# First token block of a gated attention/SwiGLU kernel: three of its four x tiles transposed by DMA instead of on TensorE

## The chip, the core and the metric

The kernel runs on one core of a Trainium2 chip, in one launch. The metric is the device time of the execution in microseconds (us). The median of several executions is the number that counts. The profiler recorded one execution, and all durations below come from that record.

## The reference, cut to what matters

The input x has 2048 tokens of 512 numbers (bf16). A linear attention block and a SwiGLU block both read it, and a gate per token mixes them:

```python
qkv = x @ wqkv                                  # 512 -> 3*512, 32 heads of 16
phi = lambda t: jnp.where(t > 0, t + 1, jnp.exp(t)) + 1e-6
pq, pk = phi(q), phi(k)
kv  = jnp.einsum("bhsd,bhse->bhde", pk, v)      # summed over all tokens
z   = jnp.einsum("bhsd->bhd", pk)
num = jnp.einsum("bhqd,bhde->bhqe", pq, kv)
den = jnp.einsum("bhqd,bhd->bhq", pq, z)[..., None] + 1e-6
a   = (num / den) @ wo
b   = (silu(x @ w1) * (x @ w3)) @ w2            # inner width 1376
g   = sigmoid((x * gate_w).sum(-1, keepdims=True))
out = g * a + (1 - g) * b
```

All of q cannot be used before k of every token has been seen, because kv and z are sums over all 2048 tokens.

## The kernel before, in words

The tokens are cut into 16 tiles of 128 (`P`) and four blocks of 512 (`TB`), so that a block has four tiles (`TPB`). The inner dimension of 512 is cut into four chunks of 128 (`KC`).

x is held twice in SBUF. `x_sb` is token-major: tokens on the partitions. `xT` is the transposed copy: the inner dimension on the partitions. A k, q, gate or up projection needs `xT`. The product `XP` (x transposed times phi(k), accumulated over all 16 tiles, from which kv comes) needs `x_sb` and phi(k).

The whole order on TensorE is written out by hand (`manual_schedule` for that engine). The start of it, which the change touches, goes so:

- `emit_warm` issues matmuls on constants ("dummies", 128 by 512, result unused). Six of them stand at the very start of TensorE's stream and two more after the first transposes.
- `emit_xT(t)` (L164 to L176) transposes tile t of the first block on TensorE: four 128x128 transposes into PSUM, two halves; DVE copies the first half to `xT` (L174) and ACT the second (L176).
- `emit_k_mm` (L178) is one of the four matmuls of k of a tile, `emit_k_phi` (L184) turns k into phi(k) on ACT and DVE and adds it to a running sum on POOL. In the first block the transposes of tiles 1 to 3 stand between the k matmuls of tiles 0 to 2.
- After the first block a loop over tiles 4 to 15 takes turns: `emit_xp(u)` (four XP matmuls of an earlier tile) and then `emit_k(t)`. So XP of tile 0 comes right before k of tile 4.

The loads are issued from two queues. The ACT queue issues the two halves of the k weights `wk_sb` (L84), then ACT loads its function table and runs a first small activation (`pre`, L88). The SP queue (`dq`) issues, strictly in order: `x_sb` tile 0 (L81), `x_sb` tile 1 (L85), `x_sb` tiles 2 and 3 (L86), and then for each of blocks 1 to 3 a DMA transpose of 512 tokens straight from DRAM into `xT` (L90) followed by the token-major copy of the same block (L94). All other weights come behind these on SP (L97 to L109): the q weights, the remainder columns with the gate, the v weights, w1, w3, wo, w2. Nothing in this stretch of the SP queue waits for a compute engine.

Later stages are: q of block 0, the last XP, kv and its product with wo, then per block the SwiGLU matmuls (`emit_ffn`), the projections of the next block, and the outputs (`emit_out`). There SP also issues DMA transposes of 128 tokens out of SBUF: `hTr` (L266) and `pqT` (L290).

Of the kernel before, what the change touches and what calls it, by code (L numbers as in the profile page):

```python
# [17 lines left out]
def kernel(  # L18
# [12 lines left out]
    nc = tc.nc  # L31
    P = nc.NUM_PARTITIONS
# [7 lines left out]
    TB = 512  # L40
    NTB = S // TB
    TPB = TB // P
# [6 lines left out]
    x2d = A_x.flatten_outer_dims()  # L49
# [14 lines left out]
    x_sb = consts.tile([P, NT, D], BF16, name="x_sb")  # L64
    xT = consts.tile([P, KC, S], BF16, name="xT")
# [13 lines left out]
    x_r = x2d.rearrange("(t p) d -> p t d", p=P)  # L79
    dq = nc.sync  # L80
    dq.dma_start(out=x_sb[:, 0:1, :], in_=x_r[:, 0:1, :])  # L81
    for i in range(2):
        kcs = slice(2 * i, 2 * i + 2)
        nc.scalar.dma_start(out=wk_sb[:, kcs, :], in_=wqkv_r[:, kcs, D : 2 * D])  # L84
    dq.dma_start(out=x_sb[:, 1:2, :], in_=x_r[:, 1:2, :])  # L85
    dq.dma_start(out=x_sb[:, 2:TPB, :], in_=x_r[:, 2:TPB, :])  # L86
    pre = consts.tile([1, 1], FP32, name="pre")
    nc.scalar.activation(out=pre[:], in_=nc.const_aps.tensor(0.0, [1, 1], FP32), func=ACT.Exp)  # L88
    for tb in range(1, NTB):
        dq.dma_start(  # L90
            out=xT[:, :, tb * TB : (tb + 1) * TB], in_=x2d[tb * TB : (tb + 1) * TB, :],
            transpose=True,
        )
        dq.dma_start(  # L94
            out=x_sb[:, tb * TPB : (tb + 1) * TPB, :], in_=x_r[:, tb * TPB : (tb + 1) * TPB, :]
# [4 lines left out]
    with nc.allow_non_contiguous_dma(reason="one gate weight per partition and chunk"):  # L100
        dq.dma_start(
            out=wr_sb[:, :, 2 * FR : NR], in_=gate_w.rearrange("(kc d o) -> d kc o", d=P, o=1)
# [14 lines left out]
        out=bm, in_=bm, pattern=[[-Dh, HPC], [0, Dh]], compare_op=ALU.is_ge, fill=0.0,  # L117
# [3 lines left out]
        out=bm, in_=bm, pattern=[[Dh, HPC], [0, Dh]], compare_op=ALU.is_ge, fill=0.0,  # L121
# [13 lines left out]
    def phi(dst, ps):  # L135
        e = work.tile([P, D], BF16, tag="phi_e", name="phi_e")
        e_ins = nc.scalar.activation(out=e[:], in_=ps, func=ACT.Exp)  # L137
        em = work.tile([P, D], BF16, tag="phi_m", name="phi_m")
        nc.vector.tensor_scalar(  # L139
            out=em[:], in0=e[:], scalar1=1.0, scalar2=1e-6, op0=ALU.min, op1=ALU.add  # L140
        )
        nc.vector.scalar_tensor_tensor(  # L142
            out=dst, in0=ps, scalar=0.0, in1=em[:], op0=ALU.max, op1=ALU.add
        )
        return e_ins
# [9 lines left out]
    def emit_warm(n):  # L155
        warm = psX.tile([P, TB], FP32, tag="XP3", name="warm")
        for i in range(n):
            nc.tensor.matmul(warm[:], lhsT=warm_l, rhs=warm_r, start=True, stop=True)

    emit_warm(6)  # L160

    st = {}

    def emit_xT(t):  # L164
        for h in range(2):
            xTp = psX.tile([P, 2, P], BF16, tag=f"XP{(2 * t + h) % 3}", name="xTp")
            for j in range(2):
                kc = 2 * h + j
                nc.tensor.transpose(  # L169
                    out=xTp[:, j, :], in_=x_sb[:, t, kc * P : (kc + 1) * P], identity=ident[:]  # L170
                )
            xT_t = xT[:, 2 * h : 2 * h + 2, t * P : (t + 1) * P]
            if h == 0:
                nc.vector.tensor_copy(out=xT_t, in_=xTp[:])  # L174
            else:
                nc.scalar.activation(out=xT_t, in_=xTp[:], func=ACT.Copy)  # L176

    def emit_k_mm(k_ps, t, kc):  # L178
        nc.tensor.matmul(  # L179
            k_ps[:], lhsT=xT[:, kc, t * P : (t + 1) * P], rhs=wk_sb[:, kc, :],  # L180
            start=(kc == 0), stop=(kc == KC - 1),
        )

    def emit_k_phi(k_ps, t):  # L184
        e_ins = phi(pk_sb[:, t, :], k_ps[:])
        if t == 0:
            nc.gpsimd.tensor_copy(pks[:], pk_sb[:, t, :])
        else:
            nc.gpsimd.tensor_add(pks[:], pks[:], pk_sb[:, t, :])  # L189
# [172 lines left out]

    k0 = [psM.tile([P, D], FP32, tag="mm", name=f"k0_{t}") for t in range(TPB)]
    emit_xT(0)
    emit_warm(2)
    emit_k_mm(k0[0], 0, 0)
    emit_k_mm(k0[0], 0, 1)
    emit_xT(1)
    emit_k_mm(k0[0], 0, 2)
    emit_k_mm(k0[0], 0, 3)  # L370
    emit_k_phi(k0[0], 0)
    emit_xT(2)
    for t in range(1, TPB):
        for kc in range(KC):
            emit_k_mm(k0[t], t, kc)
        emit_k_phi(k0[t], t)
        if t == 1:
            emit_xT(3)


    XP_ps = [psX.tile([P, D], FP32, tag=f"XP{dc}", name=f"XP{dc}") for dc in range(KC)]
# [21 lines left out]
    for c in range(KC):  # L403
# [7 lines left out]
        out=kvT_sb[:], in0=kvT_ps[:],  # L411
# [70 lines left out]
```

## Time and profile before

| what | us |
|---|---|
| median of 8 executions | 180.93 |
| lowest, highest | 180.63, 181.74 |
| the profiled execution | 180.89 |
| its span, first to last instruction | 179.1 |
| TensorE (PE) busy | 175.0, 98% of the span |
| VectorE (DVE) busy | 117.8 |
| ScalarE (ACT) busy | 66.8 |
| GpSimd (POOL) busy | 61.4 |

The profiled execution took 1.8 us more than its span: that is what lies around the first and last instruction. The rows of the profile name the line of the kernel, the engine, the operation, the tile written and the tile read. "SPq" and "ACTq" are the DMA-issuing instructions of those engines: their duration is the time that the issuing engine is held, and "us to landing" is from the start of the issue until the data is reported as arrived. A matmul's duration is modelled [...]; the distance from one start to the next is the better measure of its cost. In the chain of waits the pieces of PE stand end to end, so that a piece is listed about 0.16 us after the start of its first matmul.

### The profile page before, as it was taken

Reading aid. Unit: us, or ns where it says so; the run is one execution under the profiler, and the core shown is the slowest. Engines: PE = TensorE matmul, PEld = TensorE weight load, DVE = VectorE, ACT = ScalarE, POOL = GpSimd, SP = SyncE. Lnnn points to the kernel's source line nnn. Section 1 sums busy time; section 2 is a strip of 40 time slices with the busy share of each in tenths; the row PEclk is TensorE's granted clock in tenths of the full one; section 3 lists DMA queues with packets and bytes.
Section 4 is the critical chain, followed back from the end, with each engine's and each line's share of the span. In section 5 each row is a group of like instructions: output and inputs, shape, how many; then the busy total and the mean of one; then the engine's idle time right before and its main releaser. Section 6 shows DMA issues by size and latency. Waiting matters only on the chain.

```text
span 179.1 us, 2484 instructions
## 1 busy us (share of the span) xinstructions
PE 175.0 (98%) x892; PEld 84.1 (47%) x892; DVE 117.8 (66%) x205; ACT 66.8 (37%) x126; POOL 61.4 (34%) x69
## 2 busy tenths in 40 slices
PE   8999999999999999999999999999999999999993
PEld 3444444474444545444444444444545444444462
DVE  1578867697998837398787375978754669776000
ACT  4642322666523333342334343332433323341221
POOL 5186575646353323263003232620032328100000
PEclk9999999999999999999999999999999999999998
DMA  5999999901005010114000111240001023200011
GB/s 175 265 257 218 230 318 399 346 28 28 9 15 104 0 48 29 44 47 99 0 4 2 42 35 38 59 90 5 0 7 59 14 65 63 59 0 0 29 51 42
DMA packets 28286, 14.88 MB, mean 83 GB/s; under 512 B 19601, under 2 KB 27249, under 8 KB 28273
## 3 DMA queue, kind: packets, MB, share of 16 engines
q1 hardware_dynamic: 27728, 14.20, 29.4%
q10 hardware_dynamic: 544, 0.52, 0.9%
q8 instruction: 7, 0.11, 0.3%
q14 instruction: 7, 0.05, 0.1%
HBM read 8.42 MB, written 2.10 MB: 59 GB/s over the span
## 4 chain that ended last, share of the span: by engine, by line
PE 95%; DMA 2%; SPq 0%; DVE 0%; issue 0%; DVEq 0%
PE gate_ps L302 19%; PE o_ps L345 19%; PE up_ps L308 19%; PE o_ps L336 8%; PE XP L199 8%; PE q_ps L212 8%; PE k_ps L179 6%; PE r_ps L236 3%; DMA x_sb<-in_A_x_dram 2%; PE o_ps L340 2%; PE k L179 1%; PE kvT_ps L406 0%; PE W_ps L433 0%; PE xTp L169 0%; SPq L85 0%; SPq L81 0%
## 5 line engine op out<-in xcount | busy, mean ns | idle before, releaser
L302 PE MATMUL gate_ps<-xT,w_sb 128*128 128x512 bf16 x160 | 41.1, 379 | 0.0
L308 PE MATMUL up_ps<-xT,w_sb 128*128 128x512 bf16 x160 | 41.1, 379 | 0.0
L220 POOL TENSOR_TENSOR qz<-pq,z_sb 128x512 f32<-128x512 bf16 x16 | 18.5, 1161 | 60.6 <-DVE pq L142 58.7
L313 ACT ACTIVATE th<-gate_ps 128x512 bf16<-128x512 f32 x40 | 23.9, 597 | 38.4 <-PE gate_ps L302 38.0
L345 PE MATMUL o_ps<-w_sb,hT 128*128 128x512 bf16 (+2 forms) x180 | 37.5, 355 | 0.0
L315 DVE SCALAR_TENSOR_TENSOR gs<-th,gate_ps 128x512 bf16<-128x512 bf16 x40 | 27.3, 683 | 6.0 <-ACT th L313 5.7
L318 DVE TENSOR_TENSOR hT<-up_ps,gs 128x512 bf16<-128x512 f32 x40 | 27.6, 691 | 3.8
L139 DVE TENSOR_SCALAR phi_m<-phi_e 128x512 bf16<-128x512 bf16 x32 | 13.4, 419 | 20.7 <-ACT phi_e L137 20.5
L345 PEld LDWEIGHTS <-hT 128*128 128x128 bf16 x180 | 16.8, 97 | 17.9
L308 PEld LDWEIGHTS <-w_sb 128*128 128x128 bf16 x160 | 15.6, 98 | 19.0 <-issue 0.2
L302 PEld LDWEIGHTS <-w_sb 128*128 128x128 bf16 x160 | 15.6, 98 | 18.9 <-issue 0.3
L350 ACT ACTIVATE o_out<-o_ps,omg 128x512 bf16<-128x512 f32 (+2 forms) x17 | 11.1, 656 | 30.4 <-PE o_ps L345 30.4
L285 POOL TENSOR_TENSOR pqn<-pq,rden 128x512 bf16<-128x512 bf16 x16 | 16.6, 1056 | 14.0 <-DVE rden L278 11.7
L189 POOL TENSOR_TENSOR pks<-pks,pk_sb 128x512 f32<-128x512 f32 x15 | 17.5, 1167 | 8.9 <-DVE pk_sb L142 8.4
L223 DVE TENSOR_REDUCE den<-qz 128x32 f32<-128x512 f32 x16 | 11.0, 685 | 8.9 <-POOL qz L220 8.9
L336 PE MATMUL o_ps<-W_sb,pqT 128*128 128x512 bf16 (+2 forms) x72 | 16.8, 355 | 0.0
L212 PE MATMUL q_ps<-wq_sb,xT 128*128 128x512 bf16 x64 | 16.3, 379 | 0.0
L199 PE MATMUL XP<-pk_sb,x_sb 128*128 128x512 bf16 x64 | 16.1, 379 | 0.0
L137 ACT ACTIVATE phi_e<-k_ps 128x512 bf16<-128x512 f32 x12 | 7.2, 597 | 15.3 <-PE k_ps L179 15.3
L179 PE MATMUL k_ps<-wk_sb,xT 128*128 128x512 bf16 x48 | 12.3, 379 | 0.0
L137 ACT ACTIVATE phi_e<-q_ps 128x512 bf16<-128x512 f32 x16 | 9.6, 597 | 7.0 <-PE q_ps L212 5.8
L142 DVE SCALAR_TENSOR_TENSOR pq<-q_ps,phi_m 128x512 bf16<-128x512 f32 x16 | 11.1, 691 | 0.5
(59 smaller groups left out, 119.4 us busy)
## 6 DMA issues: line engine op xcount, KB each, us to landing
w_sb<-in_B_w_dram SPq DMA_DIRECT2D x3, 1280.0 KB, 9.6
out_dram<-o_out SPq DMA_DIRECT2D x15, 128.0 KB, 1.7
x_sb<-in_A_x_dram SPq DMA_DIRECT2D x3, 512.0 KB, 4.5
wk_sb<-in_A_wqkv_dram ACTq DMA_DIRECT2D x2, 256.0 KB, 3.5
wq_sb<-in_A_wqkv_dram SPq DMA_DIRECT2D x1, 512.0 KB, 6.6
wv_sb<-in_A_wqkv_dram SPq DMA_DIRECT2D x1, 512.0 KB, 6.6
wo_sb<-in_A_wo_dram SPq DMA_DIRECT2D x1, 512.0 KB, 10.6
x_sb<-in_A_x_dram SPq DMA_DIRECT2D x2, 128.0 KB, 2.8
```

The costliest lines, as they stand in the source:

```text
L179: nc.tensor.matmul(k_ps[:], lhsT=xT[:, kc, t * P : (t + 1) * P], rhs=wk_sb[:, kc, :], start=(kc == 0), stop=(kc == KC - 1),)
L189: nc.gpsimd.tensor_add(pks[:], pks[:], pk_sb[:, t, :])
L199: nc.tensor.matmul(XP_ps[dc][:], lhsT=x_sb[:, t, dc * P : (dc + 1) * P], rhs=pk_sb[:, t, :], start=(t == 0), stop=(t == NT - 1),)
L212: nc.tensor.matmul(q_ps[:], lhsT=xT[:, kc, ts_tok], rhs=wq_sb[:, kc, :], start=(kc == 0), stop=(kc == KC - 1),)
L220: nc.gpsimd.tensor_tensor(out=qz[:], in0=st[tb, "pq"][:, tt, :], in1=z_sb[:], op=ALU.mult)
L302: nc.tensor.matmul(gate_ps[:], lhsT=w1_sb[:, kc, fsl], rhs=xT[:, kc, tok_sl], start=(kc == 0), stop=(kc == KC - 1),)
L308: nc.tensor.matmul(up_ps[:], lhsT=w3_sb[:, kc, fsl], rhs=xT[:, kc, tok_sl], start=(kc == 0), stop=(kc == KC - 1),)
L313: nc.scalar.activation(out=th[:], in_=gate_ps[:], func=ACT.Tanh, scale=0.5)
L315: nc.vector.scalar_tensor_tensor(out=gs[:], in0=th[:], scalar=1.0, in1=gate_ps[:], op0=ALU.add, op1=ALU.mult)
L318: nc.vector.tensor_tensor(out=st[tb, "hT"][:, fc, :], in0=up_ps[:], in1=gs[:], op=ALU.mult)
L336: nc.tensor.matmul(o_ps[:], lhsT=st[tb, "pqT"][:, c, tsl], rhs=W_sb[:, c, a:b], start=(c == 0), stop=False,)
L345: nc.tensor.matmul(o_ps[:], lhsT=st[tb, "hT"][:, fc, tsl], rhs=w2_sb[:, fc, a:b], start=False, stop=(fc == FC - 1),)
```

## The change

Tiles 1 to 3 of the first block no longer go through TensorE. In the SP queue, the two loads of `x_sb` tiles 1 to 3 are replaced by two DMA transposes from DRAM into `xT`, of 128 tokens (tile 1) and of 256 tokens (tiles 2 and 3). The token-major copies of the three tiles become one DMA of 384 tokens on the ACT queue. It is written behind `emit_xT(0)`, and on ACT's own stream it stands behind `pre` and ahead of ACT's copy of tile 0's second half. The twelve TensorE transposes of tiles 1 to 3 and their six copies go away. The dummies go from six to five at the start and from two to one after tile 0's transposes. k of tiles 0 to 3 is then issued in one plain loop.

```diff
-    dq.dma_start(out=x_sb[:, 1:2, :], in_=x_r[:, 1:2, :])
-    dq.dma_start(out=x_sb[:, 2:TPB, :], in_=x_r[:, 2:TPB, :])
+    dq.dma_start(out=xT[:, :, P : 2 * P], in_=x2d[P : 2 * P, :], transpose=True)
+    dq.dma_start(out=xT[:, :, 2 * P : TB], in_=x2d[2 * P : TB, :], transpose=True)
...
-    emit_warm(6)
+    emit_warm(5)
...
     emit_xT(0)
-    emit_warm(2)
-    emit_k_mm(k0[0], 0, 0)
-    emit_k_mm(k0[0], 0, 1)
-    emit_xT(1)
-    emit_k_mm(k0[0], 0, 2)
-    emit_k_mm(k0[0], 0, 3)
-    emit_k_phi(k0[0], 0)
-    emit_xT(2)
-    for t in range(1, TPB):
+    nc.scalar.dma_start(out=x_sb[:, 1:TPB, :], in_=x_r[:, 1:TPB, :])
+    emit_warm(1)
+    for t in range(TPB):
         for kc in range(KC):
             emit_k_mm(k0[t], t, kc)
         emit_k_phi(k0[t], t)
-        if t == 1:
-            emit_xT(3)
```

## The prediction

> **What bounds the kernel now.** I read the page's first part, then the chain of waits for the first 20 us, then SP's own timeline with the rows of its DMAs.
>
> ```profile
> PE 175.0 (98%) x892; PEld 84.1 (47%) x892; DVE 117.8 (66%) x205; ACT 66.8 (37%) x126; POOL 61.4 (34%) x69
> ```
> ```profile
> 1.73 4.23 DMA x_sb<-in_A_x_dram
> 5.96 0.05 issue
> 6.01 0.40 PE xTp L169 x4
> 6.40 0.86 PE k L179 x4
> 7.27 0.22 PE xTp L169 x4
> 7.49 1.73 PE k L179 x8
> 9.22 0.86 PE XP L199 x4
> 10.08 0.86 PE k_ps L179 x4
> 10.94 0.86 PE XP L199 x4
> ```
>
> TensorE is the bound: in the chain of waits there is nothing but PE from 6.01 us on, matmuls end to end at 0.86 us per four. The last wait of PE is for `x_sb` tiles 2 and 3, issued at 1.73 and landed 4.23 us later. What is gained or lost before k of tile 4 (10.08 in the chain; its first matmul starts at 9.92 in the timeline) moves the end one for one, if nothing later begins to wait. So the whole question is: when can k of tile 4 start?
>
> That tile needs the DMA transpose of block 1, which is behind the changed lines on SP:
>
> ```profile
> 0.80 0.40 SPq L81 DMA_DIRECT2D x_sb<-in_A_x_dram  x1
> 1.26 0.42 SPq L85 DMA_DIRECT2D x_sb<-in_A_x_dram  x1
> 1.73 0.43 SPq L86 DMA_DIRECT2D x_sb<-in_A_x_dram  x1
> 2.20 3.52 SPq L90 DMA_TRANSPOSE xT<-in_A_x_dram  x1
> 5.77 0.58 SPq L94 DMA_DIRECT2D x_sb<-in_A_x_dram  x1
> 6.40 3.64 SPq L90 DMA_TRANSPOSE xT<-in_A_x_dram  x1
> ```
> ```profile
> L90 SPq DMA_TRANSPOSE xT<-in_A_x_dram x3: 3525/3641/3895, 2.2 to 10.7; - x3
> DMA to landing us min/median/max: 5.5/5.7/5.9
> ...
> L290 SPq DMA_TRANSPOSE pqT<-pqn x16: 1195/1216/1251, 52.2 to 153.0; - x16
> ...
> DMA to landing us min/median/max: 2.4/2.4/3.0
> ```
>
> SP is held 0.4 us by a plain load, but 3.5 to 3.9 us by a transpose of 512 tokens, and 1.2 us by one of 128 (`pqT`, from SBUF). Each 512-token transpose lands about 2.0 us after its issue has ended (5.5 - 3.525, 5.7 - 3.641, 5.9 - 3.895), whatever else was moving. So the issue, not the bandwidth, sets the landing. Today block 1 lands at 2.20 + 5.5 = 7.7, which leaves 2.2 us until 9.92.
>
> **The change part by part.**
>
> *TensorE work removed.* Two warm matmuls, twelve transposes. In the chain the transposes of tiles 2 and 3 are 0.40 + 0.22; tile 1's stand at 4.76 to 5.20, where k of tile 0 waits anyway: its third matmul starts at 5.20, and the second half of `wk_sb`, issued at about 1.29 with up to 3.9 us to landing, arrives just there. The dummies fill time before tile 0's data (landed at 0.80 + 2.5 = 3.3), so they cover a wait and are worth nothing. The wait at 6.0 goes. New stream: k of tile 0 ends its last two matmuls at 5.20 + 0.43 = 5.63, tile 1 follows to 6.50, tiles 2 and 3 to 8.22, XP of tile 0 to 9.08. PE could start k of tile 4 at 9.08: by itself a gain of 0.84 us. DVE loses three 0.29 us copies and ACT three of 0.38, all off the chain.
>
> *SP.* Two loads (0.42 + 0.43 us) go, two transposes come. Their cost is the deciding unknown. A line through 128 tokens = 1.22 and 512 = 3.64 gives 0.41 + 0.81 per 128 tokens: 1.22 for tile 1, 2.02 for tiles 2 and 3. Low end: cost in proportion to tokens, 3.525 / 4 = 0.88 and 1.76. High end: two pieces of 1.22 for the second, 2.45. Block 1's transpose then starts at 1.26 + 1.22 + 0.05 + 2.02 + 0.05 = 4.60 instead of 2.20 (low 4.00, high 5.03), and lands 5.5 to 5.9 later: 10.3 with the median. The matmul behind a landed load started 0.05 us after it (5.96 to 6.01), with a new weight load some 0.1 at most. So k of tile 4 starts at about 10.37, not at 9.08: PE waits 1.3 us there, and against 9.92 the sum is **+0.45**; with the shortest landing (5.5) +0.25, with the low price of the issues -0.3 to +0.1, with the high one up to +1.1. I take +0.35: between the median and shortest landing, since the transpose that was first on SP took 5.5.
>
> [...] 3.5 us against 0.58 for the same 512 KB on the same queue (L90 and L94). I go by the rows.
>
> *What is hidden by that 1.3 us wait.* Tile 1's piece (2.4 to 3.0 us by the `pqT` row) lands at 3.7 to 4.3, before 5.63. Tiles 2 and 3, issued at 2.53 and done at 4.55, land 1.2 to 2.0 us later, 5.8 to 6.6, perhaps 7.2 if their data share the DMA engines with the 384 KB from ACT, which follow `wk_sb` on ACT's queue. k of tile 2 wants them at 6.50; even 7.2 only moves XP of tile 0 to 9.8, still ahead of 10.37. ACT's new issue at 3.31 holds it for about 0.5 us (L86 and L94: 0.43 and 0.58) and so delays nothing; the dearest plain issue that I find in the trace, 2.47 us for `wv_sb` in a full queue, would hold ACT's copy of tile 0 until 6.2 and k of tile 0 until 6.7, XP of tile 0 then ends at 10.1, again under the cover. The loads from ACT land by about 8 (3.3 + 4.5) and XP of tile 1 reads them after 11. Without that cover each of these would cost its own lateness.
>
> *What is late next on SP.* Everything behind shifts by 2.4 us. Block 2's transpose would land at 14.6 (k of tile 8 starts about 17), block 3's at 19; block 1's `x_sb` at 12.8 (needed at about 16); the q weights at 24.3 (31.7); v weights 26.9 (38.2); w1 30.5 and w3 33.8 (39 and 40); wo 35.3 (43); w2 39.2 (60). SP comes free at 32.7 and its next work is ready at 39.6. All hold, so nothing is added. The copies of the three tiles on DVE and ACT and the running sum on POOL only get more room.
>
> **The sum.** The profiled execution took 180.89 (span 179.1 and 1.8 around it); plus 0.35 is 181.24, and the median stands 0.04 above that execution: 181.3.
>
> **The rivals.**
> *The short pieces are cheap to issue (gain).* No row shows a short transpose from DRAM; the 1.22 is from SBUF. If both pieces together took less than about 2.1 us, block 1 would land before 9.1 and the kernel would gain towards its floor of -0.84: 180.1. Against it: `hTr`, a quarter of the bytes of `pqT`, holds SP just as long (1.20), so a large part is a price per token or per instruction, and three 512-token issues agree to 10%. Chance 0.12, counting only gains over 0.3%.
>
> *The clock comes late (loss).* Matmuls start 0.43 us apart until 3.4 and 0.22 apart from 4.1 on: TensorE begins at half speed. The granted clock in the profile's rows says 1.00 throughout, so it cannot show the switch; the starts do. Before, PE is busy without a break from 0.84 to the switch. Now five dummies end at 2.97 and tile 0's data come at 3.37; 0.4 us are idle, 0.5 more follow before 5.2, and more at tile 2. [...] By the starts the switch stays at 4.1. [...] Chance 0.13.
>
> *The issues cost more than the line says,* by the high end or because the first transposes queue beside `wk_sb`: landing at 10.7 to 10.9, +0.8 to +1.1, so 181.7 to 182.0. Chance 0.25.
>
> **How the numbers follow.** The main case (k of tile 4 waits for block 1 at about 10.1 to 10.45, -0.1 to +0.55) has the remaining 0.50. About 0.3% (0.54 us) is what a measurement of this kernel can tell from no change. The main case counts for "same" but for a few hundredths at its upper edge; the two losses count as slower, with a few hundredths of their lower edge back in "same". Faster 0.12, same 0.48, slower 0.40. Likeliest time 181.3. The range from 180.4 to 182.2 leaves out most of the late-clock case and the lower part of the gain.
>
> **What would show it.** In SP's timeline: the two new issues at about 1.2 and 2.0 us and block 1's transpose starting near 4.6. In PE's waits: one for the DMA of `xT`, about 1.3 us, right before k of tile 4, which starts near 10.3; from there on the same unbroken stream as before. I am wrong in the gain's direction if block 1 is issued before 3.7, and in the other if matmuls after 8 us still start 0.43 apart, or if a second wait for DMA shows up behind tile 4.

## The result, and the profile after

The changed kernel is slower: a median of 184.85 us in 12 executions (181.56 to 186.16) against 181.14 for the kernel before (33 executions, 180.63 to 181.76). The ratio is 1.01, 95% interval 1.0073 to 1.0127; it leaves out the executions more than 1.5% above the fastest, which is why it is smaller than the medians say (184.85 / 181.14 = 1.02). The executions differ among themselves by 4.6 us, and those of the kernel before by 1.1. That spread is part of the answer. The first profile is of one of the long executions (185.84 us, span 184.0).

Its chain of waits for the first 30 us:

```profile
1.26 7.28 DMA xT<-in_A_x_dram
8.53 0.05 issue
8.58 5.29 PE k L179 x12
13.87 0.86 PE XP L199 x4
14.73 0.86 PE k_ps L179 x4
15.59 0.86 PE XP L199 x4
```

The last wait is no longer for block 1 but for tile 1's transpose, the one of 128 tokens: issued at 1.26, landed 7.28 us later. Then twelve k matmuls take 5.29 us. Before, they started 0.22 us apart, 2.6 us for twelve. k of tile 4 begins at 14.57 in the timeline instead of 9.92: +4.65 of the +4.95 us between the two profiled executions. From there on the stream has no wait for a DMA, as before; the other 0.3 us lie somewhere behind and are not accounted for.

TensorE's own timeline, and its waits in the first 12 us. In a row of the timeline, the brackets have the idle time before it and what ended that; in a row of the waits, the numbers are us in total, how often, and the longest:

```profile
3.89 1.01 PE L179 MATMUL k<-wk_sb,xT 128*128 128x512 bf16 x2
6.38 1.01 PE L179 MATMUL k<-wk_sb,xT 128*128 128x512 bf16 x2 [1.48 <-DMA wk_sb<-in_A_wqkv_dram]
8.58 5.29 PE L179 MATMUL k<-wk_sb,xT 128*128 128x512 bf16 x12 [1.19 <-DMA xT<-in_A_x_dram]
```
```profile
PE k L179 <- DMA wk_sb<-in_A_wqkv_dram: 1.5, 1, 1.5
PE k L179 <- DMA xT<-in_A_x_dram: 1.2, 1, 1.2
```

There are two new waits, 1.5 us for the second half of the k weights and 1.2 us for tile 1, and behind them the matmuls run at half speed (0.43 us from start to start instead of 0.22). They did so ahead of the waits too: the first two k matmuls, from 3.89 on, took 1.01 us together, against 0.59 for the two at 4.33 in the kernel before. The queues:

```profile
0.80 0.40 SPq L81 DMA_DIRECT2D x_sb<-in_A_x_dram  x1
1.26 1.29 SPq L85 DMA_TRANSPOSE xT<-in_A_x_dram  x1
2.60 1.29 SPq L86 DMA_TRANSPOSE xT<-in_A_x_dram  x1
3.94 4.93 SPq L90 DMA_TRANSPOSE xT<-in_A_x_dram  x1
```
```profile
0.80 0.98 ACTq L84 DMA_DIRECT2D wk_sb<-in_A_wqkv_dram  x2
1.81 1.28 ACT L88 ACT_TABLE_LOAD   x1 [1.81 <-issue]
1.87 0.44 ACTq L365 DMA_DIRECT2D x_sb<-in_A_x_dram  x1
```

SP issues the two pieces in 1.29 us each, and block 1 at 3.94. ACT issues the token-major load at 1.87, while its table load is still running, and not behind `pre` at 3.3. So the 384 KB are on their way almost together with tile 1's transpose. The view by microsecond shows what follows; after the stretch and its length stand the busy time of PE, its weight loads, DVE, ACT and POOL, then the granted clock, the busy share of the DMA engines and GB/s:

```profile
4.00:5.00 1.00, 0.90 (x3) 0.15 (x1) 0.00 (x0) 0.02 (x1) 0.00 (x0) 1.00 1.13 190
5.00:6.00 1.00, 0.00 (x0) 0.00 (x0) 0.00 (x0) 0.00 (x0) 0.00 (x0) 1.00 1.06 79
6.00:7.00 1.00, 0.62 (x2) 0.10 (x1) 0.00 (x0) 0.00 (x0) 0.00 (x0) 1.00 1.07 154
```

The engines are counted as busy (1.06 to 1.13) but move 79 to 190 GB/s, where plain loads in the kernel before went at 366 and 380 (3 to 5 us). The clock column says 1.00 throughout, although the matmuls start 0.43 us apart until 13.6 us, twice the 0.22 of full speed.

### The profile page after: what moved, and what is told of

Read it like the earlier page. It is cut to its first block, busy times and chain, and to the rows that moved or that the text cites. A ratio compares the mean times of both kernels' runs of the same rounds, so it can differ in the third digit from the quotient of the medians.

```text
span 184.0 us, 2451 instructions
## 1 busy us (share of the span) xinstructions
PE 177.4 (96%) x878; PEld 83.9 (46%) x878; DVE 118.7 (64%) x202; ACT 65.8 (36%) x123; POOL 61.2 (33%) x69
## 4 chain that ended last, share of the span: by engine, by line
PE 94%; DMA 4%; SPq 0%; DVE 0%; issue 0%; DVEq 0%
PE gate_ps L302 19%; PE o_ps L345 19%; PE up_ps L308 19%; PE XP L199 8%; PE o_ps L336 8%; PE q_ps L212 8%; PE k_ps L179 6%; DMA xT<-in_A_x_dram 4%; PE r_ps L236 3%; PE k L179 3%; PE o_ps L340 2%; PE kvT_ps L398 0%; PE W_ps L425 0%; SPq L81 0%; DVE o_out L354 0%
## 5 line engine op out<-in xcount | busy, mean ns | idle before, releaser
L139 DVE TENSOR_SCALAR phi_m<-phi_e 128x512 bf16<-128x512 bf16 x32 | 15.2, 475 | 26.9 <-ACT phi_e L137 26.9
L179 PEld LDWEIGHTS <-xT 128*128 128x128 bf16 x64 | 6.8, 108 | 13.1 <-issue 4.7
```

The source lines that it names most:

```text
L179: nc.tensor.matmul(k_ps[:], lhsT=xT[:, kc, t * P : (t + 1) * P], rhs=wk_sb[:, kc, :], start=(kc == 0), stop=(kc == KC - 1),)
```

## The experiments

Two things had to be told apart: what makes the data late, and what makes the matmuls slow. I had two theories for the first. "Mixing": the transposes on SP's queue and the plain load on ACT's queue disturb each other. Its rival: short transposes from DRAM are slow to land by themselves, or simply have too many bytes ahead. For the second, the theory "clock": the two waits put off the step from half speed to full speed, which came only at 13.6 us in the first profile. Its rivals: the missing dummies, or the late data alone. A "long" execution is one of the upper group of times, a "short" one of the lower. In the edits, "the changed kernel" is the starting point unless another is named. The experiments ran on three chips; each ratio is to the kernel before on the same chip, whose medians lay between 181.13 and 181.18 us.

**1. Eight and eight dummies in the two waits.**

```diff
     for t in range(TPB):
         for kc in range(KC):
+            if t == 0 and kc == 2 or t == 1 and kc == 0:
+                emit_warm(8)
             emit_k_mm(k0[t], t, kc)
```

> The changed kernel with eight dummies before the third k matmul of tile 0 and eight before k of tile 1, so that TensorE is never idle for long before 8.6 us; loads and their queues as in the change. Theory 'clock': [...] the gaps of the changed kernel put that off to about 13.6 us. Then k of tiles 1 to 3 runs with 0.22 us between starts, k of tile 4 waits for block 1's transpose (landed at 10.8 in the profile of the change) and starts near 10.9: 181.8 to 182.1 us, with a spread under 1 us. Theory 'landing': the late data alone cost the time and the clock would be there anyway: 183 to 186 us as in the changed kernel, or more for the dummies.

Measured: 184.23 us (183.24 to 184.48, 4 executions), ratio 1.0151 (1.0125 to 1.0176). Neither expectation: the k matmuls of tiles 1 to 3 started 0.22 us apart, but I had given too many dummies.

```profile
6.69 0.43 PE k L179 x2
7.12 1.75 PE warm L158 x8
8.86 2.59 PE k L179 x12
11.45 0.86 PE XP L199 x4
```

In this chain of waits the dummies themselves are the path: the third k matmul followed the first eight at 6.52 without a wait for the weights, tile 1 had landed at 7.4, and the dummies held PE until 8.7. The speed is read off the x12 row (2.59 against 5.29). It does not show that the dummies brought it: full speed was there from the matmul at 4.56 on, and the first of the sixteen dummies started at 4.78. So this run decides nothing between the theories.

**2. The token-major load on SP, behind the two short transposes.**

```diff
     dq.dma_start(out=xT[:, :, 2 * P : TB], in_=x2d[2 * P : TB, :], transpose=True)
+    dq.dma_start(out=x_sb[:, 1:TPB, :], in_=x_r[:, 1:TPB, :])
...
-    nc.scalar.dma_start(out=x_sb[:, 1:TPB, :], in_=x_r[:, 1:TPB, :])
```

> The changed kernel with the token-major load of tiles 1 to 3 on SP, between the transpose of 256 tokens and that of block 1, instead of on the ACT queue. Theory 'mixing': transposes and plain copies from two queues at once slow each other far below the rate of either alone (about 100 to 130 GB/s between 4.6 and 6.6 us in the profile of the change). With only the k weights beside it, tile 1's transpose lands before 6 us instead of 8.5, the k weights at about 5.5 instead of 6.4, block 1 (issued at about 4.4) at about 10.1: 181.0 to 182 us if the clock then comes at once, up to 184 where it does not. Rival 'short transposes from DRAM are slow to land by themselves': tile 1 still lands 7 us after its issue, 183 to 186 us.

Measured: 180.80 us (180.43 to 181.50, 17 executions), ratio 0.998 (0.9967 to 0.9992). This one move takes away the whole loss and a little more. Tile 1 lands 4.3 us after its issue, at 5.6. The rows of its transpose, in the changed kernel and then here:

```profile
L85 SPq DMA_TRANSPOSE xT<-in_A_x_dram x1: 1292/1292/1292, 1.3 to 1.3; - x1
DMA to landing us min/median/max: 7.3/7.3/7.3
```
```profile
L85 SPq DMA_TRANSPOSE xT<-in_A_x_dram x1: 1280/1280/1280, 1.3 to 1.3; - x1
DMA to landing us min/median/max: 4.3/4.3/4.3
```

TensorE's timeline in this run:

```profile
4.44 3.98 PE L180 MATMUL k<-wk_sb,xT 128*128 128x512 bf16 x16
8.26 1.03 PE L200 MATMUL XP<-pk_sb,x_sb 128*128 128x512 bf16 x4
9.53 1.04 PE L180 MATMUL k_ps<-wk_sb,xT 128*128 128x512 bf16 x4 [0.25 <-DMA xT<-in_A_x_dram]
```

All sixteen k matmuls stand nearly end to end, and k of tile 4 waits for block 1 (landed at 9.5) as the prediction's main case had it, only earlier. It starts at 9.53 instead of 9.92. The expectation's 10.1 was too late because block 1's issue took 2.85 us here.

**3. Only the dummies, in the kernel before.**

```diff
-    emit_warm(6)
+    emit_warm(5)
...
-    emit_warm(2)
+    emit_warm(1)
```

> The kernel before with five dummies at the start and one after tile 0's transposes, as in the change; nothing else changed. Theory 'clock by dummies': the missing dummies alone leave a gap of 0.4 us [...]: +1 us or more and a spread of some us. Theory 'clock by waits': the gap of 0.4 us is harmless and only the long waits of the change (1.5 and 1.2 us) put the clock off: 181.1 us, same spread as before.

Measured: 181.12 us (180.92 to 181.80, 14 executions), ratio 1.0001 (0.9989 to 1.0013). One dummy fewer in each of the two places costs nothing by itself.

**4. All early loads in one queue.** The two halves of `wk_sb` are issued on SP too, behind tile 0:

```diff
-        nc.scalar.dma_start(out=wk_sb[:, kcs, :], in_=wqkv_r[:, kcs, D : 2 * D])
+        dq.dma_start(out=wk_sb[:, kcs, :], in_=wqkv_r[:, kcs, D : 2 * D])
...
     dq.dma_start(out=xT[:, :, 2 * P : TB], in_=x2d[2 * P : TB, :], transpose=True)
+    dq.dma_start(out=x_sb[:, 1:TPB, :], in_=x_r[:, 1:TPB, :])
...
-    nc.scalar.dma_start(out=x_sb[:, 1:TPB, :], in_=x_r[:, 1:TPB, :])
```

> The changed kernel with all early loads on SP, in the order tile 0, both halves of the k weights, the two short transposes, the token-major load of tiles 1 to 3, block 1: no second queue beside the transposes. Theory 'mixing': no stretch under 250 GB/s between 3 and 7 us; k weights land by 4.7, tile 1 (issued at about 2.2) by 5.5, tiles 2 and 3 by 6.8, block 1 (issued at about 5.3) near 11: 181.9 to 182.3 us if the clock comes by 7.5. Rival 'short transposes from DRAM are slow by themselves': tile 1 lands at 9 or later, 184 us or more.

Measured: 181.57 us (181.30 to 182.43, 20 executions), ratio 1.0026 (1.0016 to 1.0036). Tile 1 lands 3.7 us after its issue, the shortest of all, at 5.9. The expectation that no stretch falls under 250 GB/s did not hold (128 between 4.5 and 5.0, 125 between 6.0 and 6.5), so a low rate alone is no sign of two queues. Block 1 is issued a microsecond later than in the second experiment and lands at 10.4; k of tile 4 starts at 10.49, and that is the time lost. Full speed came late here too, at about 6.6, hidden under that wait for block 1. That was only 1.2 us behind the end of a wait of 0.3 us:

```profile
5.40 3.79 PE L180 MATMUL k<-wk_sb,xT 128*128 128x512 bf16 x14 [0.29 <-DMA wk_sb<-in_A_wqkv_dram]
```

So not every gap keeps full speed away: in this profile one of 0.3 us did not.

**5. The changed kernel once more, beside the others.** 

> The changed kernel as it is, once more, beside the others on one chip. Both theories: 183 to 186 us in most executions. What differs from execution to execution should be when the short transposes land (8.5 us for tile 1 in the first profile, 7.4 us with the same loads in the run with eight and eight dummies) and how long k of tiles 1 to 3 runs with 0.43 us between starts.

Measured: 183.53 us (181.66 to 184.91, 10 executions), ratio 1.0083 (1.0045 to 1.012). Four executions at 181.66 to 181.97, six at 183.42 to 184.91, nothing between. The profile is of the fastest:

```profile
4.08 0.61 PE L179 MATMUL k<-wk_sb,xT 128*128 128x512 bf16 x2
5.22 0.59 PE L179 MATMUL k<-wk_sb,xT 128*128 128x512 bf16 x2 [0.53 <-DMA wk_sb<-in_A_wqkv_dram]
6.99 2.76 PE L179 MATMUL k<-wk_sb,xT 128*128 128x512 bf16 x12 [1.18 <-DMA xT<-in_A_x_dram]
9.59 1.03 PE L199 MATMUL XP<-pk_sb,x_sb 128*128 128x512 bf16 x4
10.46 0.38 PE L179 MATMUL k_ps<-wk_sb,xT 128*128 128x512 bf16 x1
```

Here full speed came at about 4 us, the twelve matmuls took 2.60 from the first start to XP's, and k of tile 4 started at 10.46. Against the first profile (14.57) that is 4.11 us less: 1.59 by the earlier landing of tile 1 (6.99 instead of 8.58) and 2.5 by the speed. The speed differed before the first wait: at 4.08 it was there in this execution, at 3.89 and 4.27 in the first profile it was not, although TensorE had then been at work since 0.84 with no gap over 0.1 us. So the waits do not decide alone: in this execution full speed had come before them and outlasted both (0.53 and 1.18 us). Two losses are added in the change: late data, in both profiles, and the late clock, in one of them and, judged by the two groups of times, in most executions.

**6. Three and six dummies in the waits.**

```diff
         for kc in range(KC):
+            if t == 0 and kc == 2:
+                emit_warm(3)
+            if t == 1 and kc == 0:
+                emit_warm(6)
             emit_k_mm(k0[t], t, kc)
```

> The changed kernel with three dummies before the third k matmul of tile 0 and six before k of tile 1, which end at about 7 us and so before tile 1's transpose has landed (7.4 to 8.5 us); the run with eight and eight had them end at 8.9 and made them the path. Theory 'clock': k of tiles 1 to 3 runs with 0.22 us between starts; XP of tile 0 ends near 11 and k of tile 4 starts at 10.9 to 11.5: 182 to 182.7 us, at least 2 us under the changed kernel on the same chip. Theory 'landing': no gain over the changed kernel.

Measured: 182.12 us (181.56 to 184.69, 11 executions), ratio 1.0052 (1.0032 to 1.0072), 1.4 us under the changed kernel on the same chip by the medians; expected were 2 at least. Ten of eleven stayed under 183.2, where six of ten of the changed kernel were above 183.4; the loads are the same in both. The profile fell on the eleventh: there tile 0 itself landed at 4.36 (3.3 in the kernel before), the gap ahead of it was 1.3 us, and the matmuls stood 0.43 us apart until 9.5. These dummies come after that gap and cannot fill it.

**7. The token-major load on SP ahead of the transposes.**

```diff
+    dq.dma_start(out=x_sb[:, 1:TPB, :], in_=x_r[:, 1:TPB, :])
     dq.dma_start(out=xT[:, :, P : 2 * P], in_=x2d[P : 2 * P, :], transpose=True)
...
-    nc.scalar.dma_start(out=x_sb[:, 1:TPB, :], in_=x_r[:, 1:TPB, :])
```

> The changed kernel with the token-major load of tiles 1 to 3 on SP ahead of the two transposes instead of on the ACT queue, so that the same bytes stand ahead of tile 1's transpose, but in its own queue. Theory 'mixing': the plain load and the transposes follow each other; tile 1 (issued at about 1.7) lands by 6.6, block 1 (issued at about 4.5) by 10: 180.9 to 181.8 us. Theory 'bytes ahead': what delays tile 1 is only the 384 KB ahead of it; it lands at 7.4 or later here too, and the time stays at 183 us or more.

Measured: 181.80 us (180.82 to 183.24, 20 executions), ratio 1.0039 (1.0013 to 1.0066). Tile 1 lands at 6.5, block 1 at 9.1. Against the second experiment (5.6) the bytes ahead cost 0.9 us by themselves. But with the same bytes ahead, in the same queue, tile 1 is 0.4 to 2 us earlier than in the four profiles with the load on ACT (7.0 to 8.5), so bytes are a part of the delay and not all of it. The times, however, fall into two groups of ten: 180.82 to 181.24, and 182.35 to 183.24. The profile is of the upper group: at 4.28 and 4.70 two k matmuls started 0.42 apart, then TensorE waited 0.8 us for the k weights (landed at 6.07), and the matmuls stood 0.43 apart until 10.3.

```profile
1.29 4.78 DMA wk_sb<-in_A_wqkv_dram
6.07 0.04 issue
6.11 5.40 PE k L180 x14
```

**8. The same, with three dummies in that gap.**

```diff
         for kc in range(KC):
+            if t == 0 and kc == 2:
+                emit_warm(3)
             emit_k_mm(k0[t], t, kc)
```

> The version with the token-major load ahead of the transposes on SP (times in two groups, 180.8 to 181.2 and 182.4 to 183.2 us), plus three dummies before the third k matmul of tile 0. They end by 6.0 us even at half speed, so they delay nothing: that matmul waited until 6.1 for the second half of the k weights. Theory 'clock': the upper group is the executions in which the gap from 4.9 to 6.1 put off the full speed; with the gap filled it disappears, nearly all executions at 180.8 to 181.5 us. Rival 'the two groups come from the loads': both groups stay.

Measured: 181.01 us (180.79 to 181.72, 12 executions), ratio 1.0001 (0.9985 to 1.0017). The upper group is gone: none of twelve executions, where it had ten of twenty without the three dummies. The loads are untouched, and the dummies do no useful work. The two versions ran on two chips, but the kernel before took 181.13 us on one and 181.15 on the other. The profile shows an execution in which full speed was there at 4.24, before the dummies (4.68):

```profile
4.24 0.61 PE L180 MATMUL k<-wk_sb,xT 128*128 128x512 bf16 x2
4.68 0.81 PE L159 MATMUL warm<-const-bfloat16-1.0 128*128 128x512 bf16 x3
6.42 3.18 PE L180 MATMUL k<-wk_sb,xT 128*128 128x512 bf16 x14 [0.93 <-DMA wk_sb<-in_A_wqkv_dram]
```

Here the dummies did not even fill the gap: 0.93 us of it remained (the weights landed at 6.38), and the fourteen matmuls stayed at full speed. So the profile is not the evidence; the group that is gone is. Together with the sixth experiment it is the best evidence that gaps on TensorE put off the clock: in both, only dummies were added and most of the long executions went.

**9. Two dummies at the start, in the best version.** The second experiment's kernel, with

```diff
-    emit_warm(5)
+    emit_warm(2)
```

> The version with the token-major load on SP behind the 256-token transpose (180.8 us, one group), with two dummies at the start instead of five. The loads are the same, so all data land as before; only TensorE idles from 1.7 to 3.5 us, before any work could start. Theory 'clock': full speed comes later in many executions, k of tiles 0 to 3 runs with 0.43 us between starts and overruns block 1's landing at 9.5: 182 to 183 us in those. Rival 'the dummies do nothing': 180.8 us, one group.

Measured: 181.29 us (180.65 to 182.32, 16 executions), ratio 1.0004 (0.9987 to 1.0022). Not two groups but a wider spread; the median is 0.5 us above that version's 180.80 (on another chip), and the two intervals overlap by a little. The profile (182.32) has 0.43 us between starts until 9.3. It points the way of "clock" and would not carry it alone.

**10. One load moved in the kernel before.** Block 1's token-major copy on ACT's queue:

```diff
-        dq.dma_start(
+        (nc.scalar if tb == 1 else dq).dma_start(
             out=x_sb[:, tb * TPB : (tb + 1) * TPB, :], in_=x_r[:, tb * TPB : (tb + 1) * TPB, :]
```

> The kernel before with one load moved: the token-major copy of block 1 is issued on the ACT queue (right behind the k weights, at about 1.9 us) instead of on SP behind block 1's transpose. Nothing else changed. Theory 'mixing': it meets block 1's transpose on the DMA engines; the rate in the stretch where both move falls below 200 GB/s (290 to 370 when they follow each other), and block 1's transpose lands after 9 us instead of 7.7. Theory 'bytes ahead': it lands about 1.4 us later at most (512 KB at 370 GB/s) with the rate at 290 or more. In the time: 181 to 182.5 us by both, as tiles 2 and 3 of block 0 may land later too.

Measured: 181.79 us (180.99 to 182.22, 20 executions), ratio 1.0027 (1.0014 to 1.004). Block 1's transpose landed 7.9 us after its issue, at 10.1 instead of 7.7; the plain load landed at 8.6. That is a microsecond later than the 9.1 that the bytes alone would allow by my estimate (7.7 plus 1.4 for 512 KB at 370 GB/s). The rate where both move:

```profile
6.00:7.00 1.00, 0.37 (x3) 0.02 (x2) 0.14 (x1) 0.94 (x2) 0.00 (x0) 1.00 1.14 346
7.00:8.00 1.00, 1.00 (x8) 0.61 (x9) 0.66 (x3) 0.38 (x1) 0.00 (x0) 1.00 1.19 165
8.00:9.00 1.00, 1.00 (x10) 0.56 (x8) 0.81 (x3) 0.72 (x2) 0.41 (x1) 1.00 1.25 232
```

So it falls below 200 here too, but that proves nothing: in the kernel before, the same microsecond has 127 GB/s, with the engines less busy (0.79 instead of 1.19).

```profile
7.00:8.00 1.00, 1.00 (x10) 0.54 (x8) 0.81 (x3) 0.70 (x2) 0.39 (x1) 1.00 0.79 127
```

What is left as evidence is the landing of block 1. The time was lost elsewhere: tiles 2 and 3 of block 0, a plain load on SP, landed at 6.9 instead of 5.96, and k of tile 4 started at 10.9, after block 1 had come. So a plain load came later as well, though by 1.0 us and thus no more than the added bytes would allow (1.4).

**11. One transpose of 384 tokens.** The second experiment's kernel, with the two short transposes as one:

```diff
-    dq.dma_start(out=xT[:, :, P : 2 * P], in_=x2d[P : 2 * P, :], transpose=True)
-    dq.dma_start(out=xT[:, :, 2 * P : TB], in_=x2d[2 * P : TB, :], transpose=True)
+    dq.dma_start(out=xT[:, :, P : TB], in_=x2d[P : TB, :], transpose=True)
```

> The version with the token-major load on SP behind the transposes, with one transpose of 384 tokens instead of 128 and 256. Issue costs measured so far: 1.29 us for 128 and for 256 tokens, 2.8 to 3.6 for 512. If 384 tokens take about 2.0, block 1 is issued at about 4.0 instead of 4.56 and lands at 8.9 to 9.0, tile 1 lands at about 6.0 instead of 5.6: k of tile 4 starts at about 9.3 instead of 9.5, 180.5 to 180.8 us. If 384 cost 2.6 or more, it is no better than the two pieces: 180.8 to 181.2 us.

Measured: 181.07 us (180.99 to 181.31, 12 executions), ratio 1.0001 (0.9989 to 1.0013). The issue took 1.58 us, less than I expected, and block 1 was issued at 3.52 and landed at about 9.1. But tile 1 now lands with the other two, at 6.38, and k of tile 1 waits for it: k of tile 4 starts at 9.89. The wait has moved from block 1 to tile 1. The two pieces look better (180.80), but on another chip and with intervals that overlap.

The version of the second experiment is the only one that beats both kernels: 0.2% under the kernel before (interval 0.1 to 0.3%).

## Why the prediction was wrong, point by point

**"What is hidden by that 1.3 us wait" failed, at tile 1.** Of the 4.65 us by which k of tile 4 came late in the first profile, about 2.1 are late data (less what the removed work gave) and 2.5 the late clock (further down). The prediction put tile 1's landing at 3.7 to 4.3, from the row of `pqT`. Measured with the load on ACT: 8.5, 7.4, 7.0 and 7.7 in four profiles; in the second experiment, 5.6. So the cover of a wait for block 1 was not there: PE waited for tile 1, in the first profile until 8.58. The row taken was of a transpose from SBUF, later in the kernel (the first ones at 52 to 57 us, with 0 to 131 GB/s moving), and the place where it stood had two queues at work.

Behind this is a rule that the prediction drew from too few rows: a transpose lands 2.0 us after its issue has ended, "whatever else was moving", so "the issue, not the bandwidth, sets the landing". For the transposes of 512 tokens that held in the changed kernel too (block 1: issue ended at 8.87, landed at 10.86). But there the issue itself stretched: it took 3.3 us in one execution and 4.9 in another of the same program. The short issues stayed at 1.29 us, and tile 1 landed 2.4 us (fourth experiment) to 6.0 us (first profile) after the end of its own.

In the four profiles the ACT load landed (1.87 plus 6.4, 5.2, 4.8 and 5.6) at 8.3, 7.1, 6.7 and 7.5: each time 0.3 us ahead of tile 1. It looks as if the transpose were not complete until the load beside it is through. That the order of the queues matters is shown by the second and the seventh experiment: of the 1.3 to 2.9 us between 5.6 and the four landings, 0.9 come with the bytes ahead, and 0.4 to 2.0 only with the second queue (one profile each for the 5.6 and the 6.5). Why the transpose is held back, no run shows. Nor is it settled why the rate fell to 79 GB/s in the first profile: in the fast execution of the same program it was 337 in the same microsecond.

**The same part failed on ACT's issue.** It was placed at 3.31, behind `pre`, because the order on ACT's stream says so. It ran at 1.87, beside the table load, and at 1.87 to 1.9 in the three other profiles with this load on ACT. So its place in the stream did not give the time of its issue. The prediction did weigh what the load's data would do to tiles 2 and 3 ("perhaps 7.2"; measured 9.2 and 7.6), but not what it would do to tile 1.

**The k weights.** "Arrives just there", 5.20, was taken over from the kernel before. The matmul that needs them started at 6.38 in the long execution and at 5.22 in the short one.

**The issue costs were wrong in the other direction.** The line through 128 and 512 tokens gave 1.22 and 2.02. Measured: 1.29 and 1.29. Block 1 was issued at 3.94 rather than 4.60. Its landing, "10.3", was 10.9 in the long execution (the issue took 4.93 us) and 9.3 in the short one (3.34). In neither did k of tile 4 wait for it. The main case did occur in the second experiment, with -0.4 instead of +0.35.

**The clock was named, and mis-sized.** The rival expects the right effect, but gave it a chance of 0.13. The sign that the prediction named for it, matmuls after 8 us still 0.43 apart, was there: in the first profile the switch to 0.22 came at 13.6, and the slow matmuls cost 2.5 us on top of the late data. I counted gaps of 0.4 and 0.5 us. In the first profile the 0.4 was not there (tile 0 landed at 2.95), the 0.5 became a wait of 1.5, and one of 1.2 was new. How long work must last before the switch, no run shows: from the end of the last wait to the switch it was 5.0 us in the first profile, 5.1, 4.2 and 3.8 in those of the sixth, seventh and ninth experiment, and 1.2 in that of the fourth. Why the speed was there at 4.08 in one execution and not at 4.27 in another of the same program stays open too. What is shown is that dummies in the waits make most of the long executions go away (one of eleven left in the sixth experiment, where the changed kernel had six of ten; none of twelve in the eighth, where it was ten of twenty without them): that is how the late data cost twice.

**Right:** one dummy fewer in each place costs nothing by itself (third experiment); the shift of everything behind on SP is covered (no later wait for a DMA on TensorE, although the q weights were issued at 18.0 instead of 15.3); transposes are not as fast as plain loads (1.29 us of issue against 0.42, and in the kernel before 290 GB/s from 6 to 7 us, where a transpose moves, against 366 to 380 from 3 to 5, where plain loads do); and once the data are there, the removed transposes do give TensorE a nearly unbroken start (second experiment).

## What to carry to other kernels

When a transposing DMA stands at the start of the critical path, issue large loads that are not urgent behind it on its own queue, not beside it on another (here tile 1 landed at 5.6 us instead of 7.0 to 8.5), and look up in the trace when that load is really issued (1.87 here, where the order of the stream suggested 3.3). A wait at the start of a kernel can be paid twice, since TensorE may stay at half speed behind it (2.5 us here); count the distance between matmul starts, not the clock column, and fill a wait that cannot be removed with dummies that end before it does. When the times of one kernel fall into two groups, profile one of each before explaining the median.

## What was not expected of the hardware

- A transpose of 128 and one of 256 tokens from DRAM hold SP equally long, 1.29 us; 384 tokens 1.58; 512 tokens 2.1 to 5.5.
- Once there, full speed survived gaps: in the short execution of the changed kernel TensorE had 0.53 and 1.18 us of idle time right behind the switch and stayed at 0.22 us between starts. Before the switch, a wait of 0.8 to 1.7 us went with a switch at 9.3 to 10.3 us in three profiles, and the two waits of the change with one at 13.6; waits of 0.3 us and less went with a switch at 6.6 (fourth experiment).
- The issue of a 512-token transpose took 3.3 us in one execution of the changed kernel and 4.9 in another, and the transpose landed 2.0 us after its end in both.
- A DMA that stands behind a table load and an activation on ACT's stream was issued 0.06 us after the table load had begun (1.87 and 1.81 in the first profile).
